# Key moments formed once and spread by a product, a later gate, another pair order and another order of loads in a gated mix of attention and gMLP

## The chip, the cores and the metric

One core of a Trainium2 chip runs the kernel. TensorE (PE) multiplies matrices into eight PSUM banks, VectorE (DVE) and ScalarE (ACT) read them, GpSimd (POOL) works on SBUF alone, and SyncE (SP) issues every transfer of this kernel in one queue. The metric is the device time of one execution in microseconds; lower is better.

## What is computed

The input x (2048 x 512) goes through two blocks, and a gate per row mixes their outputs:

```python
g = _sigmoid((x * gate_w).sum(-1, keepdims=True))
# a: attention with 32 heads of 16 for q, one shared k and v
scores = jnp.einsum('bhqd,bkd->bhqk', q, k) * Dh ** (-0.5)
o = jnp.einsum('bhqk,bkd->bhqd', _softmax(scores, axis=-1), v)
a = o.transpose(0, 2, 1, 3).reshape(B, S, H * Dh) @ wo
# b: gMLP, F = 1376, Fh = 688
z = _gelu(jnp.einsum('bsd,df->bsf', x, w_in))
z2 = _layernorm(z[..., Fh:], axis=-1)
gg = jnp.einsum('ts,bsf->btf', w_sp, z2) + b_sp[None, :, None]
b = jnp.einsum('bsf,fd->bsd', z[..., :Fh] * gg, w_out)
return g * a + (1 - g) * b
```

## The kernel before

Scores are small, so the kernel replaces exp(s) by a polynomial of third degree in s. All heads share k and v, and the sums over keys of 1, k, k k and k k k, each with and without v, are small tables, the moments. Per query only products of q with these tables are left. A guard compares the largest |q| |k| with a bound, and a general path (not run here) stands behind it.

The work is a list of tasks (`Plan.add`): engine, estimated duration, what is read and written, a priority. A planner (`Plan.run`) plays the list through with its own estimates and gives every engine a fixed order; the order of the instructions is thus set before the run, and a wait on an engine holds all that stands behind it there. `after` adds a true dependency, with its semaphore wait.

*Start.* `g_x(c)` (L551) transposes four chunks of x, 512 rows each, by TensorE into `xT`. `g_kv(c)` (L561) multiplies them with k's and v's weights and with the gate's vector as a 33rd column, and DVE forms, per key, `kx` (k), `RK` (k times v, k, v, 1) and `psi`: products of pairs of k's 16 components. There are 128 pairs (r, r+i) with i from 0 to 7, in the order r outermost (L53). POOL forms `kkE`, the pairs at distance 8, and `kkD`, a correction for the squares. `moments(c)` (L593) sums over keys: per tile of 128 keys two matmuls into bank 5 (L598, L599), and three products, each as four matmuls of 32 columns side by side with the same weights, into bank 4 (L600 to L602), so that each of four groups of 32 rows holds the same table. `moments_out` (L604) scales them into `T3`, `T3d`, `M2`, `T1b`, `T2b`, `TEb`.

*Gate.* `g_gate(c)` (L626) computes the gate once more, as rows, with weights `gwr`; `gate_out` (L631) takes the exponentials on ACT. The first gelu waits for them (`after=[ex_t[0]]`, L746), since the two functions need different tables on ACT.

*Queries.* `g_q(u)` (L640) makes q for unit u: 512 rows and 8 heads, of 16 units. q is written to DRAM (`qe`, L652; the DRAM pattern is 2 x 16 rows of 512), its first 8 rows are copied behind them (L654), and `y_load` (L659) reads it back twice for each half e of the unit: `Y` has the component r of a pair in every one of 128 partitions, `YB` the component r+i. The DRAM patterns are 16 x 8 rows of 2048.

*Units.* `unit(u)` (L671): for e in 0, 1 and j in 0 to 3, POOL multiplies Y by YB to X (L691), TensorE multiplies T3 with X (`W`, L696), DVE multiplies the result by Y to Pr (L698). M2 and T3d products of the four X, and `sel` products of the four Pr, are summed into the numerator N and the denominator D (L702 to L711). `g_den` (L717) divides and rescales for each of four row groups, `tg`.

*gMLP.* `g_z2` and `g_z1` multiply x by the two halves of w_in with gelus; layer norm on DVE, its root by a power on POOL (L752), and a normalising pass on ACT (L756). `g_sp` multiplies by the transposed w_sp, which `ld_wT` loads; `g_out` multiplies by wo and w_out and writes the rows out. z1, z2, sp and out products are the matmuls that fill TensorE while a unit waits.

Most products run as four matmuls of 32 output columns each, side by side in TensorE (`mm4`, `mmq`, L477 and L487), fewer over the whole width (`mm1`). The trace names helpers: L480, L485 and L490 are all matmuls of `mm4`, `mm1` and `mmq`.

The main list (L835 to L883): the four chunks with their moments and gates, then q for units 0 to 3, all z2, all z1, then per `tg` its four units with q four units ahead, the denominators, sp and out.

Of the kernel before, what the change touches and what calls it, by code (L numbers as in the profile page):

```python
# [17 lines left out]
D = 512  # L18
NH = 32
DH = 16  # L20
F = 1376
# [13 lines left out]
WARM = 5  # L35
# [7 lines left out]
SLACKS = {("pool", "pe"): 1200.0, ("dve", "pe"): 350.0, ("act", "pe"): 300.0}  # L43
# [3 lines left out]
DMA_ISSUE = 300.0  # L47


def constants():  # L50
# [22 lines left out]
    for e in range(2):  # L73
        for t in range(2):
            sel[p, e, t, 16 * e + 8 * t + p % 8] = 1
# [4 lines left out]
    rol = np.eye(128) + bmq * ((p[:, None] + 8) % 16 == p[None, :] % 16)  # L80
# [4 lines left out]
    small = np.concatenate([sel.reshape(128, 128), hsel.reshape(128, 128), bmq, rol], 1)  # L85
# [103 lines left out]
class Task:  # L189
    __slots__ = ("alt", "fn", "deps", "users", "left", "pri", "grp", "first", "dma", "bytes", "chan", "tag", "idx",  # L190
                 "ready", "eng", "start", "end", "op", "rate", "opens", "gates")


class Plan:
# [8 lines left out]
    def add(self, eng, cost, fn, r=(), w=(), pri=50.0, grp=None, evac=False, dma=0, size=0, chan=None, rate=DMA_RATE, tag="", after=(), opens=()):  # L203
# [5 lines left out]
        t.users, t.op, t.eng = [], None, None  # L209
        r, w = list(r), list(w)  # L210
# [16 lines left out]
        t.gates = []  # L227
        for d in t.deps:
            d.users.append(t)
        for d in t.opens:  # L230
            d.users.append(t)
        t.left = len(t.deps) + len(t.opens)
# [8 lines left out]
    def run(self, prog, allowed):  # L241
# [5 lines left out]
        pipe = [0.0]  # L247
        busy = {e: 0.0 for e in ENG}
# [9 lines left out]
        def enter(t):  # L258
            for e in t.alt:
                rt = max([0.0] + [d.end + (lat(d, e) if not (d.eng == e == "pe") else 0.0) for d in t.deps + t.opens])  # L260
                cand[e].append((rt, t))
# [29 lines left out]
        while done < len(self.tasks):  # L291
# [23 lines left out]
            for rt, t in cand[e]:  # L315
# [10 lines left out]
                k = (t.pri, t.idx)  # L326
# [4 lines left out]
            cost, fn = t.alt[e]  # L331
            t.eng = e
# [10 lines left out]
            if t.dma:  # L343
                free[e] = now + cost
                st = max(pipe[0], now + DMA_ISSUE)
                pipe[0] = st + t.bytes / t.rate
# [24 lines left out]
def build_kernel(nc, x_d, wq_d, wk_d, wv_d, wo_d, win_d, wsp_d, bsp_d, wout_d, gw_d, out_d):  # L371
    es = ExitStack()
    with es:
# [32 lines left out]
        cs = sb("cs", [128, 512], B16)  # L406
# [10 lines left out]
        T1d = sb("T1d", [128, 1], F32)  # L417
        S0 = sb("S0", [128, 1], F32)
# [45 lines left out]
        rol = cs[:, 384:512]  # L464
        x2 = x_d.rearrange("b s d -> (b s) d")
        out2 = out_d.rearrange("b s d -> (b s) d")

        def diag(t):

            a = t[:, :, :]  # L470
            return bass.AP(tensor=a.tensor, offset=a.offset, ap=[a.ap[0], [48, 2], [1, 16]])
# [4 lines left out]

        def mm4(b, n, off, lhsT, rhs, start, stop):  # L477

            def f(t):
                return [t.matmul(ps[32 * q:32 * q + 32, 512 * b() + off:512 * b() + off + n], lhsT[:, 32 * q:32 * q + 32], rhs,  # L480
                                 start=start, stop=stop, tile_position=(0, 32 * q)) for q in range(4)]
            return f

        def mm1(b, n, off, lhsT, rhs, start, stop):
            return lambda t: t.matmul(bank(b(), n, off), lhsT, rhs, start=start, stop=stop)  # L485

        def mmq(b, n, off, lhsTs, rhss, start, stop):  # L487

            def f(t):
                return [t.matmul(ps[32 * q:32 * q + 32, 512 * b() + off:512 * b() + off + n], lhsTs[q], rhss[q],  # L490
                                 start=start, stop=stop, tile_position=(0, 32 * q)) for q in range(4)]
            return f
# [8 lines left out]
        nd = [0]  # L501

        def load(eng, fn, w, r=(), size=0, n=1, pri=0.0, chan=None, rate=DMA_RATE, tag="", after=()):
# [3 lines left out]
            return add(eng, 4500.0 if rate < DMA_RATE else 540.0 * n, fn, r=r, w=w, dma=16 * n, size=size, pri=pri, chan=chan, rate=rate, tag=tag, after=after)  # L507
# [8 lines left out]
        add("dve", 350.0, lambda v: v.memset(Pr[:, 0, 0, :], 0.0), w=[("Pr", 0)], pri=-1)  # L516
        gw_ = Group("any")
# [17 lines left out]
        load("sp", lambda q: q.dma_start(win[:, :, 0:FH], win_d[:, 0:FH].rearrange("(dt p) n -> p dt n", p=128)), ["win1"], size=704512, pri=6)
        add("pool", 300.0, lambda g: g.memset(bspz[:], 0.0), w=[("bspz", 0), ("bspz", 1)], pri=0)
        add("pool", 100.0, lambda g: g.memset(nhalf[:], -0.5), w=["nhalf"], pri=0)
        add("pool", 100.0, lambda g: g.memset(RK[:, :, 304:305], 1.0), w=["rk1"], pri=0)
        add("pool", 1600.0, lambda g: g.memset(kkD, 0.0), w=[("X", c) for c in range(4)], pri=0)
# [8 lines left out]
        add("dve", 100.0, lambda v: v.tensor_copy(gwr[:], wkvg[:, :, 32:33].broadcast_to([128, 4, 32])), r=["gw"], w=["gwr"], pri=0)  # L548
# [12 lines left out]
        def g_kv(c):  # L561
            g = Group("any")
            for k in range(4):
                for dt in range(4):
                    add("pe", 26.0, mm1(lambda g=g: g.b, 33, 64 * k, xT[:, dt, 512 * c + 128 * k:512 * c + 128 * k + 128], wkvg[:, dt, 0:33], dt == 0, dt == 3),
                        r=["wk", "wv", "gw", ("x", c, dt)], grp=g, pri=0, tag="kv")
# [5 lines left out]
            add("dve", 200.0, lambda v: v.tensor_copy(RK[:, t4, 272:304].rearrange("p k (e d) -> p k e d", e=2),  # L572
                                                      src()[:, :, 16:32].unsqueeze(2).broadcast_to([128, 4, 2, 16])),
                w=[("rv", c)], grp=g, evac=True, pri=0, tag="rv")
            add("dve", 130.0, lambda v: v.tensor_scalar(RK[:, t4, 256:272], src()[:, :, 0:16], 0.25, None, ALU.mult), w=[("rk", c)], grp=g, evac=True, pri=0, tag="rk")
            add("dve", 100.0, lambda v: v.tensor_scalar(gs[:, t4].unsqueeze(2), src()[:, :, 32:33], E_MAX, None, ALU.min), w=[("gs", c)], grp=g, evac=True, pri=0, tag="gs")
            kxa = kx[:, t4, 0:16]
            kxo = bass.AP(tensor=kxa.tensor, offset=kxa.offset, ap=[kxa.ap[0], [32, 4], [1, 16], [1, 8]])
            add("dve", 620.0, lambda v: v.tensor_tensor(psi[:, t4, :].rearrange("p k (r i) -> p k r i", i=8), kxa.unsqueeze(3).broadcast_to([128, 4, 16, 8]), kxo, ALU.mult),
                r=[("kx", c)], w=[("psi", c)], pri=1, tag="psi")  # L580
            add("dve", 1150.0, lambda v: v.tensor_tensor(RK[:, t4, 0:256].rearrange("p k (c d) -> p k c d", d=16), kxa.unsqueeze(3).broadcast_to([128, 4, 16, 16]),
# [554 lines left out]
```

## Time and profile before

| | us |
|---|---|
| runs | 338.77, 335.24, 338.85 |
| median | 338.77 |
| profiled execution | 337.39 |
| its span | 335.6 |

The profile is of one execution; the span runs from the first instruction to the last. "Issue" in a chain of waits is time in which an engine waited for nothing that the profile shows. A granted clock of 1.00 is TensorE's full speed. The DMA share is the mean busy share of the core's 16 DMA engines. In a row of a group there stand the count, then busy time and mean nanoseconds of one instruction, then the engine's idle time before them and what ended it.

### The profile page before, as it was taken

To read this page: it belongs to the slowest core of one execution; us is meant where nothing else is said; L and a number is where in the kernel's file an instruction comes from. 1 tells how busy PE (TensorE), PEld (TensorE's weight loads), DVE (VectorE), ACT (ScalarE), POOL (GpSimd) and SP (SyncE) were. 2 spreads that over 40 slices of the span, in tenths; PEclk is the share of its full clock that TensorE was granted. 3 is DMA by queue.
4 is the path that set the end of the run, shared out by engine and by line. 5 is a ranking of instruction groups with operands and counts; after the bars stand their busy time and mean duration, and the time that the engine had idled before them with its cause. 6 is when DMAs were issued, how large, how long until landed. Compare 5 with 4: busy or idle time off the path is not lost.

```text
span 335.6 us, 13852 instructions
## 1 busy us (share of the span) xinstructions
PE 303.2 (90%) x6279; PEld 162.9 (49%) x6279; DVE 239.7 (71%) x335; ACT 93.8 (28%) x163; POOL 165.9 (49%) x156
## 2 busy tenths in 40 slices
PE   5976879899999997999999769988999999799993
PEld 2763345454445554564445335542565554244551
DVE  1855479998465798876949859849588977949522
ACT  2525467966655010113212002230100012000001
POOL 7421049656757284367484614376672487640000
PEclk9977899999999999999999999999999999999998
DMA  6956264999996899398999752988987579700002
GB/s 160 348 160 170 72 130 120 190 199 283 189 215 156 199 165 237 94 189 158 263 187 233 185 120 42 238 187 209 248 153 177 109 177 240 172 5 2 4 4 66
DMA packets 54472, 54.17 MB, mean 161 GB/s; under 512 B 36900, under 2 KB 45960, under 8 KB 54280
## 3 DMA queue, kind: packets, MB, share of 16 engines
q1 hardware_dynamic: 54408, 53.24, 68.6%
q8 instruction: 50, 0.82, 1.1%
q14 instruction: 14, 0.11, 0.1%
HBM read 40.65 MB, written 5.24 MB: 137 GB/s over the span
## 4 chain that ended last, share of the span: by engine, by line
PE 74%; DVE 12%; issue 6%; ACT 4%; DMA 1%; SPq 1%; DVEq 0%
PE ps L480 61%; PE ps L490 8%; DVE Pr L698 6%; PE ps L485 3%; ACT z L756 2%; PE ps L762 2%; DMA wkvg<-in_gate_w_dram 1%; ACT z L745 1%; DVE bst L747 1%; DVE z L801 1%; DVE win L735 0%; DVE nmr L753 0%; DVE Prd L713 0%; DVE Rh L728 0%; DVE outsb L828 0%
## 5 line engine op out<-in xcount | busy, mean ns | idle before, releaser
L691 POOL TENSOR_TENSOR X<-Y,YB 128x512 bf16<-128x512 bf16 x128 | 148.3, 1159 | 96.1 <-DMA Y<-qe 36.2
L698 DVE TENSOR_TENSOR Pr<-ps,Y 128x1024 bf16<-128x1024 f32 x128 | 152.3, 1215 | 32.3 <-issue 22.7
L480 PE MATMUL ps<-wT,z 128*32 128x512 bf16 x1280 | 85.0, 379 | 0.0
L480 PE MATMUL ps<-X,T 128*32 128x512 bf16 x1024 | 80.7, 380 | 4.1 <-DVE Pr L698 3.9
L480 PEld LDWEIGHTS ps<-wT,z 128*32 128x32 bf16 x1280 | 36.6, 97 | 30.0 <-issue 0.2
L480 PEld LDWEIGHTS ps<-X,T 128*32 128x32 bf16 x1024 | 26.9, 96 | 31.8 <-DVE Pr L698 12.6
L480 PE MATMUL ps<-win,xT 128*32 128x344 bf16 x512 | 25.0, 320 | 3.4 <-ACT z L745 2.9
L480 PE MATMUL ps<-wout,z 128*32 128x512 bf16 x384 | 26.2, 379 | 0.5 <-DVE z L804 0.5
L679 ACT ACTIVATE E<-ps 128x512 bf16<-128x512 f32 x16 | 9.5, 597 | 59.8 <-PE ps L480 56.1
L712 ACT ACTIVATE Ns<-ps 128x512 f32<-128x512 f32 x16 | 9.6, 599 | 58.1 <-PE ps L490 58.1
L648 ACT ACTIVATE Qt<-ps 128x512 bf16<-128x512 f32 x16 | 9.6, 597 | 47.2 <-PE ps L480 38.2
L827 ACT ACTIVATE outsb<-ps,G 128x512 bf16<-128x512 f32 x14 | 9.5, 687 | 41.5 <-PE ps L480 41.5
L480 PE MATMUL ps<-xT,win 128*32 128x512 bf16 x320 | 20.3, 380 | 0.5 <-ACT E L679 0.5
L801 DVE TENSOR_TENSOR z<-ps,z 128x512 bf16<-128x512 f32 x20 | 13.7, 683 | 9.7 <-PE ps L480 9.5
L490 PE MATMUL ps<-Pr,cs 128*32 128x512 bf16 x256 | 19.7, 379 | 0.5 <-DVE Pr L698 0.5
L735 DVE SCALAR_TENSOR_TENSOR win<-Ns,S,ps 128x512 bf16<-128x512 f32 x16 | 11.9, 745 | 10.9 <-PE ps L480 10.8
L480 PEld LDWEIGHTS ps<-win,xT 128*32 128x32 bf16 x512 | 12.6, 99 | 14.1 <-ACT z L745 7.0
L480 PE MATMUL ps<-xT,wq 128*32 128x512 bf16 x256 | 18.1, 400 | 0.6 <-ACT Q L656 0.2
L747 DVE BATCH_NORM_STATS2 bst<-z 128x6 f32<-128x344 bf16 x32 | 15.4, 505 | 4.0 <-ACT z L745 3.9
L480 PE MATMUL ps<-wo,win 128*32 128x512 bf16 x256 | 17.8, 379 | 0.0
L745 ACT ACTIVATE z<-ps 128x344 bf16<-128x344 f32 x32 | 14.0, 454 | 9.0 <-PE ps L480 7.9
L756 ACT ACTIVATE z<-z,nmr,rstd 128x688 bf16<-128x688 bf16 x16 | 15.0, 960 | 1.7 <-DVE nmr L753 1.6
(119 smaller groups left out, 314.6 us busy)
## 6 DMA issues: line engine op xcount, KB each, us to landing
Y<-qe SPq DMA_DIRECT2D x32, 512.0 KB, 5.2
YB<-qe SPq DMA_DIRECT2D x32, 512.0 KB, 6.7
wT<-in_A_x_dram SPq DMA_DIRECT2D x4, 512.0 KB, 6.1
qe<-Qt SPq DMA_DIRECT2D x64, 32.0 KB
out_dram<-outsb SPq DMA_DIRECT2D x16, 128.0 KB, 3.3
win<-in_B_w_in_dram SPq DMA_DIRECT2D x2, 688.0 KB, 8.8
qe<-qe SPq DMA_DIRECT2D x16, 64.0 KB
wout<-in_B_w_out_dram SPq DMA_DIRECT2D x1, 640.0 KB, 5.3
```

What stands on the lines that cost most here:

```text
L480: return [t.matmul(ps[32 * q:32 * q + 32, 512 * b() + off:512 * b() + off + n], lhsT[:, 32 * q:32 * q + 32], rhs, start=start, stop=stop, ...
L485: return lambda t: t.matmul(bank(b(), n, off), lhsT, rhs, start=start, stop=stop)
L490: return [t.matmul(ps[32 * q:32 * q + 32, 512 * b() + off:512 * b() + off + n], lhsTs[q], rhss[q], start=start, stop=stop, tile_position=( ...
L648: add({"act": (520.0, lambda a: a.activation(Qt[:, s, :], bank(g.b), ACT.Copy))}, 0, None, w=[("Q", s)], grp=g, evac=True, pri=1, tag="Qev")
L691: xf = lambda v, xi=xi, j=j, n=n: v.tensor_tensor(X[:, xi, :], Y[:, n % NY, j, :], YB[:, n % NYB, j, :], ALU.mult)
L698: add("dve", 1230.0, lambda v, gw=gw, pi=pi, n=n, j=j: v.tensor_tensor(Pr[:, pi, :, :], bank(gw.b, 1024).rearrange("p (t n) -> p t n", t=2 ...
L712: add({"act": (590.0, lambda a: a.activation(Ns[:, u % NNS, :], bank(gn.b), ACT.Copy))}, 0, None, w=[("Ns", u % NNS)], grp=gn, evac=True, ...
L735: add("dve", 750.0, lambda v, gr=gr, u=u, G=G: v.scalar_tensor_tensor(OT[:, tg % 2, G, :], Ns[:, u % NNS, :], S0[:, 0:1], bank(gr.b), ALU. ...
L745: add("act", 400.0, lambda a, g=g, h=h: a.activation(z2[:, FH * st + 344 * h:FH * st + 344 * h + 344], bank(g.b, 344), ACT.Gelu_apprx_tanh ...
L747: add("dve", 495.0, lambda v, h=h: v.bn_stats(bst[:, st, h, :], z2[:, FH * st + 344 * h:FH * st + 344 * h + 344]), r=[("z2", st, h)], w=[( ...
L756: add("act", 820.0, lambda a, s2=s2: a.activation(z2[:, FH * s2:FH * s2 + FH], z2[:, FH * s2:FH * s2 + FH], ACT.Identity, bias=nmr[:, s2:s ...
L801: add("dve", 690.0, lambda v: v.tensor_tensor(dst, bank(g.b), dst, ALU.mult), w=[("z1", ft, tc)], grp=g, evac=True, pri=3.5, tag="u")
```

## The change

- The moments in bank 4 are no longer formed in four copies. `RK` holds the distance-8 pairs ahead of its other columns, and a whole-width matmul takes 128 columns of it as weights: two matmuls for a key tile where three groups of four stood, and one into bank 5 where two stood. `moments_out` splits the result into two bf16 parts (`mT`) and spreads it over the partitions by six matmuls with 0/1 tables `spr`.
- The E row becomes (q_r - q_(r+8)) squared in place of the sum, `TEb` changes its sign, and the correction of the squares goes into 16 rows of M2 (`m2c`). `kkE` and `kkD` as tiles are gone; DVE or POOL may form psi and k v.
- The pairs are ordered by i first. `sel`, `psi`, T3 and both DRAM patterns of `y_load` follow: 8 x 16 rows of 2048 in place of 16 x 8.
- The gate's vector is loaded late, its column is a product of its own (`g_gs`, 64 matmuls of one column), the gate's products come after z1 in the list, the exponentials after all gelus. ACT's gelu table is asked for at the start.
- Loads: wq before x1, win1 after unit 0's loads, Q writes and Y loads with priorities of their own. `hold` only says that a task is planned after another; it replaces `after` for late loads.
- M2 and T3d products wait for the quad's last Pr. Q is computed three units ahead, two units first.
- Planner: a price for a change between four-tile and whole-width matmuls and a preference against it, a higher rate for the first loads, slack for L752 and for ACT to SP. Nine warm-up matmuls instead of five.

```diff
-    pairs = [(r, (r + i) % 16) for r in range(16) for i in range(8)]
+    pairs = [(r, (r + i) % 16) for i in range(8) for r in range(16)]
...
-                add("pe", c_mm(288), mm1(lambda: gK3.b, 288, 0, psi[:, kt, :], RK[:, kt, 0:288], st, False), r=[("psi", c), ("rkv", c), ("rk", c), ("rv", c)], grp=gK3, pri=1, tag="K3")
-                add("pe", 26.0, mm1(lambda: gK3.b, 16, 272, kkD[:, kt, :], RK[:, kt, 272:288], False, sp_), r=[("X", c), ("rv", c)], grp=gK3, pri=1, tag="K3")
-                add("pe", 30.0, mmq(lambda: gT.b, 49, 0, rep(kx[:, kt, :]), rep(RK[:, kt, 256:305]), st, False), r=[("kx", c), ("rk", c), ("rv", c), "rk1"], grp=gT, pri=1, tag="T")
-                add("pe", 26.0, mmq(lambda: gT.b, 16, 64, rep(kkE[:, kt, :]), rep(RK[:, kt, 272:288]), False, False), r=[("kkE", c), ("rv", c)], grp=gT, pri=1, tag="T")
-                add("pe", 26.0, mmq(lambda: gT.b, 1, 96, rep(RK[:, kt, 272:304]), rep(RK[:, kt, 304:305]), False, sp_), r=[("rv", c), "rk1"], grp=gT, pri=1, tag="T")
+                add("pe", c_mm(288), mm1(lambda: gK3.b, 288, 0, psi[:, kt, :], RK[:, kt, 16:304], st, sp_), r=[("psi", c), ("rkv", c), ("rk", c), ("rv", c)], grp=gK3, pri=1, tag="K3")
+
+                add("pe", 30.0, mm1(lambda: gT.b, 49, 0, RK[:, kt, 193:321], RK[:, kt, 272:321], st, False), r=[("rkv", c), ("rk", c), ("rv", c), "rk1"], grp=gT, pri=1, tag="T")
+                add("pe", 26.0, mm1(lambda: gT.b, 16, 49, RK[:, kt, 0:128], RK[:, kt, 288:304], False, sp_), r=[("kkE", c), ("rkv", c), ("rv", c)], grp=gT, pri=1, tag="T")
...
+            for i, (off, lo, n) in enumerate(((0, 0, 49), (64, 49, 16), (96, 48, 1))):
+                for z in range(2):
+                    add("pe", 30.0, lambda t, i=i, off=off, lo=lo, n=n, z=z: t.matmul(bank(gT2.b, n, off), spr[:, i, :], mT[:, z, lo:lo + n], start=i == 0 and z == 0, stop=i == 2 and z == 1),
+                        r=["cs", "mTh", "mTl"], grp=gT2, pri=1, tag="T2")
...
+        def g_gs(st):
+            for dt in range(4):
+                add("pe", 26.0, mm1(lambda: gS.b, 1, st, xT[:, dt, 128 * st:128 * st + 128], wkvg[:, dt, 32:33], dt == 0, dt == 3), r=["gw", ("x", st // 4, dt)], grp=gS, pri=22, tag="gate")
...
-            load("sp", lambda q: q.dma_start(Y[:, n % NY, :, :].rearrange("p j n -> p (j n)"), dap(qe, o0, [[QP, 16], [0, 8], [1, 2048]])), [("Y", n % NY)], r=[("qe", u)],
-                 size=524288, pri=10 + u + 0.1 * e, chan="y%d" % (n % NY), tag="Y")
-            yld[0] = load("sp", lambda q: q.dma_start(YB[:, n % NYB, :, :].rearrange("p j n -> p (j n)"), dap(qe, o0, [[QP, 16], [QP, 8], [1, 2048]])), [("YB", n % NYB)], r=[("qe", u), ("qx", u)],
-                 size=524288, pri=10 + u + 0.2 * e, chan="yb%d" % (n % NYB), tag="YB")
+            load("sp", lambda q: q.dma_start(Y[:, n % NY, :, :].rearrange("p j n -> p (j n)"), dap(qe, o0, [[0, 8], [QP, 16], [1, 2048]])), [("Y", n % NY)], r=[("qe", u)],
+                 size=524288, pri=YPRI + u + 0.1 + 0.4 * e, chan="y%d" % (n % NY), tag="Y")
+            yld[0] = load("sp", lambda q: q.dma_start(YB[:, n % NYB, :, :].rearrange("p j n -> p (j n)"), dap(qe, o0, [[QP, 8], [QP, 16], [1, 2048]])), [("YB", n % NYB)], r=[("qe", u), ("qx", u)],
+                 size=524288, pri=YPRI + u + 0.2 + 0.4 * e, chan="yb%d" % (n % NYB), tag="YB")
...
-                add("pe", c_mm(512), mmq(lambda: gn.b, 512, 0, [M2[:, e, :]] * 4, [X[:, i, :] for i in xs], False, False), r=["M2"] + xr, grp=gn, pri=pr_, tag="N")
+                add("pe", c_mm(512), mmq(lambda: gn.b, 512, 0, [M2[:, e, :]] * 4, [X[:, i, :] for i in xs], False, False), r=["M2"] + xr, grp=gn, pri=pr_, tag="N", after=tp[3:])
```

More of the change, by code (lines that the diff above doesn't have):

```diff
@@ L34 @@
 SLACK = 1.016
-WARM = 5
+WARM = 9
 QP = 4096 + 256
@@ L190 @@
     __slots__ = ("alt", "fn", "deps", "users", "left", "pri", "grp", "first", "dma", "bytes", "chan", "tag", "idx",
-                 "ready", "eng", "start", "end", "op", "rate", "opens", "gates")
+                 "ready", "eng", "start", "end", "op", "rate", "opens", "gates", "tiles", "slack")
 class Plan:
@@ L226, in add @@
         t.opens = [self.lastw[k] for k in opens]
-        t.gates = []
+        t.gates = list(hold)
+        t.slack = slack
         for d in t.deps:
             d.users.append(t)
-        for d in t.opens:
+        for d in t.opens + t.gates:
             d.users.append(t)
-        t.left = len(t.deps) + len(t.opens)
+        t.left = len(t.deps) + len(t.opens) + len(t.gates)
         for k in r:
@@ L247, in run @@
         pipe = [0.0]
+        tiles = 1
         busy = {e: 0.0 for e in ENG}
@@ L325, in run @@
                     continue
-                k = (t.pri, t.idx)
+                k = (t.pri + (SWITCH_PRI if e == "pe" and t.tiles != tiles else 0.0), t.idx)
                 if best is None or k < best[0]:
@@ L331, in run @@
             cost, fn = t.alt[e]
+            if e == "pe":
+                if t.tiles != tiles:
+                    cost += SWITCH
+                tiles = t.tiles
             t.eng = e
@@ L345, in run @@
                 st = max(pipe[0], now + DMA_ISSUE)
-                pipe[0] = st + t.bytes / t.rate
+                pipe[0] = st + t.bytes / (DMA_FIRST if st < 16000.0 and t.rate == DMA_RATE else t.rate)
                 t.end = pipe[0] + DMA_LAT
@@ L475, in build_kernel, with mm1 @@
         add = pl.add
+        def mm1(b, n, off, lhsT, rhs, start, stop):
+            return lambda t: t.matmul(bank(b(), n, off), lhsT, rhs, start=start, stop=stop)
         def mm4(b, n, off, lhsT, rhs, start, stop):
@@ L481, in f @@
                                  start=start, stop=stop, tile_position=(0, 32 * q)) for q in range(4)]
+            f.tiles = 4
             return f
-        def mm1(b, n, off, lhsT, rhs, start, stop):
-            return lambda t: t.matmul(bank(b(), n, off), lhsT, rhs, start=start, stop=stop)
         def mmq(b, n, off, lhsTs, rhss, start, stop):
@@ L501, in build_kernel, with load @@
         nd = [0]
-        def load(eng, fn, w, r=(), size=0, n=1, pri=0.0, chan=None, rate=DMA_RATE, tag="", after=()):
+        yld = [None]
+        def load(eng, fn, w, r=(), size=0, n=1, pri=0.0, chan=None, rate=DMA_RATE, tag="", after=(), hold=()):
             if chan is None:
@@ L516, in build_kernel @@
         add("dve", 350.0, lambda v: v.memset(Pr[:, 0, 0, :], 0.0), w=[("Pr", 0)], pri=-1)
+        add("act", 1300.0, lambda a: a.activation(nmr[:, 0:1], ones[:, 0:1], ACT.Gelu_apprx_tanh), r=["ones"], w=["junk2"], pri=-2, tag="table")
         gw_ = Group("any")
@@ L863, in build_kernel @@
             g_z2(st)
-        for ft in range(6):
-            for tc in range(4):
-                g_z1(ft, tc)
         for tg in range(4):
@@ L870, in build_kernel @@
                 unit(u)
-                if u < 2:
-                    ld_wT(u)
+                if u == 0:
+                    ld_win1()
+                    for ft in range(6):
+                        for tc in range(4):
+                            g_z1(ft, tc)
+                    load("sp", nonc(lambda q: q.dma_start(wkvg[:, :, 32:33], gw_d.rearrange("(dt p one) -> p dt one", p=128, one=1))), ["gw"], size=16384, pri=20, hold=[yld[0]])
+                    add("dve", 100.0, lambda v: v.tensor_copy(gwr[:], wkvg[:, :, 32:33].broadcast_to([128, 4, 32])), r=["gw"], w=["gwr"], pri=20, tag="gate")
+                    for c in range(4):
+                        g_gate(c)
+                    for st in range(NST):
+                        g_gs(st)
+                    gate_out()
+                    q_and_guard(2)
+                if u in (1, 3):
+                    ld_wT(u // 2)
                 if u == 2:
                     ld_late()
-                if u + 4 < 16:
-                    q_and_guard(u + 4)
+                if u + 3 < 16:
+                    q_and_guard(u + 3)
             g_den(tg)
```

160 lines of the change are left out of this document (85 added, 75 removed).

## The prediction

> **What bounds the kernel now.** I read the page first: the shares, the slices, the queues, the chain.
>
> ```profile
> span 335.6 us, 13852 instructions
> PE 303.2 (90%) x6279; PEld 162.9 (49%) x6279; DVE 239.7 (71%) x335; ACT 93.8 (28%) x163; POOL 165.9 (49%) x156
> ...
> PEclk9977899999999999999999999999999999999998
> ...
> q1 hardware_dynamic: 54408, 53.24, 68.6%
> q8 instruction: 50, 0.82, 1.1%
> ...
> PE 74%; DVE 12%; issue 6%; ACT 4%; DMA 1%; SPq 1%; DVEq 0%
> ```
>
> TensorE is busy for 90% and carries 74% of the chain: the kernel is bound by matmuls, and a gain must come from time in which TensorE works badly or not at all. The profiled run took 337.39 us, of which the span is 335.6; the median of the three runs is 338.77, 1.4 above it. My sum is made against 337.4.
>
> Then the table by stretches tells where TensorE loses time.
>
> ```profile
> core 0: us, PE busy (x) PEld busy (x) DVE busy (x) ACT busy (x) POOL busy (x), PEclk, DMA share, GB/s
> 10.00:20.00 10.00, 8.17 (x207) 6.24 (x206) 7.75 (x17) 4.87 (x10) 3.63 (x4) 0.96 0.77 256
> 20.00:30.00 10.00, 7.57 (x240) 5.68 (x237) 5.99 (x14) 3.96 (x7) 3.19 (x4) 0.84 0.67 185
> 30.00:40.00 10.00, 8.38 (x128) 4.01 (x132) 5.21 (x23) 4.76 (x10) 0.00 (x0) 0.68 0.46 121
> 40.00:50.00 10.00, 7.66 (x184) 3.75 (x172) 6.37 (x17) 6.04 (x13) 3.38 (x4) 1.00 0.51 110
> 41.00:42.00 1.00, 0.84 (x20) 0.45 (x24) 0.10 (x1) 0.86 (x3) 0.00 (x0) 1.00 0.13 46
> 119.00:121.00 2.00, 2.00 (x56) 1.20 (x52) 1.96 (x3) 0.53 (x2) 1.65 (x2) 1.00 0.93 272
> 50.00:295.00 245.00, 230.74 (x4718) 121.00 (x4722) 192.42 (x234) 69.15 (x120) 146.22 (x127) 1.00 0.82 183
> ```
>
> From 50 to 295 us TensorE idles for 14.3 of 245 us. From 10 to 50 it idles for 8.2 of 40, and where it is busy the granted clock was 0.84 in one stretch and 0.68 in the next. So the time to be won lies in the first 50 us. The chain of waits and the timeline say what stands there.
>
> ```profile
> 2.79 4.65 DMA wkvg<-in_gate_w_dram
> ...
> 16.76 1.83 issue
> ...
> 27.57 3.13 issue
> ```
>
> ```profile
> 7.46 0.45 DVE L548 COPY gwr<-wkvg 128x128 bf16<-128x128 bf16 x1 [3.78 <-DMA wkvg<-in_gate_w_dram]
> ...
> 10.71 0.68 PE L485 MATMUL ps<-wkvg,xT 128*128 128x33 bf16 x13
> ...
> 13.71 0.64 PE L490 MATMUL ps<-wT 128*32 128x16 bf16 x48
> ...
> 24.96 0.49 PE L480 MATMUL ps<-win,xT 128*32 128x344 bf16 x8
> ...
> 27.05 1.28 ACT L745 ACT_TABLE_LOAD   x1
> ...
> 29.63 1.20 SPq L664 DMA_DIRECT2D YB<-qe  x2
> ...
> 46.23 1.04 POOL L752 TENSOR_TENSOR rstd<-ve,nhalf 128x4 f32<-128x4 f32 x1 [19.51 <-DVE ve L751]
> ...
> 47.50 4.85 POOL L691 TENSOR_TENSOR X<-Y,YB 128x512 bf16<-128x512 bf16 x4 [0.23 <-POOL rstd L752]
> ```
>
> The two "issue" gaps are waits of TensorE for nothing that the profile shows, both inside the run of small moment matmuls. My reading, not shown by these rows: its instructions had not arrived (the q8 row is their fetch, 0.82 MB in 50 packets). The first z2 matmuls stand at 24.96, since their gelu may run only after the gate's exponentials. GpSimd stood for 19.5 us behind an early L752, so the first X came at 47.50.
>
> **The change, part by part.**
>
> *Moments.* Per key tile there were 1 + 1 + 4 + 4 + 4 = 14 matmuls (L598 to L602), now 3, for 16 tiles: 176 fewer, each with its weight load.
>
> ```profile
> L485 PE MATMUL ps<-wT,X 128*128 128x16 bf16 x16 | 2.8, 187 | 0.0
> ...
> L490 PE MATMUL ps<-wT 128*32 128x49 bf16 x64 | 2.6, 186 | 0.0
> ...
> L490 PE MATMUL ps<-wT 128*32 128x1 bf16 x64 | 2.4, 166 | 1.8 <-issue 1.8
> ...
> L490 PE MATMUL ps<-wT 128*32 128x16 bf16 x64 | 2.2, 174 | 3.1 <-issue 3.1
> ...
> L618 DVE SCALAR_TENSOR_TENSOR T2b<-ps,cs 128x128 bf16<-128x128 f32 x1 | 0.3, 292 | 3.1 <-PE ps L490 3.1
> ```
>
> A run of 48 small ones took 0.64 us, 53 ns for each four. Three fours per tile go (159 ns) and two single ones come, at 34 to 52 ns by the 0.68 us for 13 L485 matmuls: about 65 ns saved, and some 30 ns for the 16-column product; 16 x 95 = -1.5 us. With the run three times shorter I let both gaps go: -5.0. (If they come back elsewhere: 0.) The low clock follows them: 10 x 0.16 + 10 x 0.32 = 4.8 us of clock are lost in the two stretches; I take all of it back as part of the same step, -4.8, lower end 0, since work then also finds fewer free slots. [...]
>
> *The spread.* Six matmuls over `mT` with two DVE steps before them lengthen the way from moments to T1b, T2b, TEb. By a small DVE step of this kernel (L618 below) that is two times 0.3 us and the matmuls, about 1 us; z2 matmuls hide it. Without that cover +1.
>
> *Gate late.* The scalar load of 512 single elements held DVE until 7.46 us, and its copy took 0.45; the xT copies behind it (from 7.60) stood ready for about as long: -0.7, lower end 0, upper -1.2. The gate's 64 four-tile matmuls only move. The one column that rode along in the key/value product becomes 64 matmuls of its own: 64 x 34 to 52 ns = 2.2 to 3.3; +2.5. They stand in the full stretch, so nothing hides them. The exponentials and their 1.28 us table load move to ACT behind the last gelu; ACT is busy for 69 of 245 us there, and the first reader is far behind: 0. Its cover gone, +2.
>
> *Longer warm-up.* Four more matmuls while TensorE waits for x: 0.
>
> *Order of loads, POOL.* wq before x1 delays x1 by one 512 KB load, but the gate's load is gone and win1 is moved away; L752 is no longer ahead of X.
>
> ```profile
> SPq L165 <- DVE Pr L698: 58.5, 17, 9.5
> ...
> SPq L652 <- ACT Q L656: 34.6, 10, 13.3
> ```
>
> The first YB was issued at 29.63, behind a write of Qt that itself waited; the queue lost 34.6 us in such waits. Now the loads of units 0 and 1 come ahead of the later Q writes, and wq arrives earlier: I put the first YB at about 19 us, a head start of 11 us for the loads, and the first X some 15 to 20 us earlier. A wait of SP for a Q that is late now delays Y and YB behind it, as before. Its worth is only that TensorE has more to choose from; 0, lower end -4.
>
> *N and D of a quad in one run.* M2 and T3d products now wait for the fourth Pr (1215 ns, L698 below). z1, sp and out work is queued to fill in; X buffers come free later, while GpSimd idles for 96 us before L691 (its row below). 0; without cover a quarter of a Pr for each of 32 quads, +10; in the best case -2.
>
> *Staying in one tiling.* I see no idle time at changes of tiling in the rows above; 0 to -2, taken as 0.
>
> *Y and YB by another order.* This is the part that can cost.
>
> ```profile
> L691 POOL TENSOR_TENSOR X<-Y,YB 128x512 bf16<-128x512 bf16 x128 | 148.3, 1159 | 96.1 <-DMA Y<-qe 36.2 <-PE ps L490 27.2 <-PE ps L480 24.8
> L698 DVE TENSOR_TENSOR Pr<-ps,Y 128x1024 bf16<-128x1024 f32 x128 | 152.3, 1215 | 32.3 <-issue 22.7 <-PE ps L480 8.6 <-PE ps L490 0.4
> ...
> Y<-qe SPq DMA_DIRECT2D x32, 512.0 KB, 5.2
> YB<-qe SPq DMA_DIRECT2D x32, 512.0 KB, 6.7
> ...
> qe<-Qt SPq DMA_DIRECT2D x64, 32.0 KB
> ```
>
> The bytes stay, but the DRAM side goes from 16 rows of 8 to 8 of 16. In 41 to 42 us only the writes of Qt (L652) are in flight; their DRAM pattern begins with a dimension of 2, and the share is 0.13, that is 2 of 16 engines, at 46 GB/s, 23 each. In 119 to 121 Y loads run, whose pattern begins with 16: share 0.93, 272 GB/s, 18.3 per engine. So a pattern that begins with 8 should use 8 engines. From 50 to 295 us 183 x 245 = 44.8 MB are moved, of which 58 Y and YB loads are 30.4 MB. The eight engines would carry 30.4/8 + 14.4/16 = 4.70 MB each, and the two that also write Qt (2.1 MB) 5.62. They have 245 + 11 = 256 us. At 23 GB/s the two need 244 us, at 18.3 they need 307: 0 to +51. Below nothing I see no reason. I take 23, since eight engines ask for less in all (184 GB/s) than the 272 that pass now; but at 95% use some waits for Y must come: +2.
>
> [...]
>
> Sum: 337.4 - 1.5 - 5.0 - 4.8 - 0.7 + 2.5 + 2 = 329.9; I say 330.
>
> **The rivals.**
>
> *A. The loads become the bound (slower).* Place: POOL X L691 waiting for Y and YB, already 36.2 us now. It begins where an engine under load moves less than 5.62 MB / 256 us = 22.0 GB/s, and eats the gain of 9.5 us at 5.62/265.5 = 21.2. Between that and today's 18.3 (middle 19.7: 285 us, +29) the time is 337.4 - 9.5 + 29 = 357; at 18.3 it is 379. For: 16 engines do only 18.3 now, and the matmul order is fixed, so a late Y stalls TensorE. Against: half as many engines compete.
>
> *B. The loads cost nothing* (16 engines after all, or hidden), and the earlier X saves its 4 us as well: 337.4 - 9.5 - 4 = 324.
>
> *C. The start does not shorten:* ACT, with 16 normalising passes and 32 gelus early, ends the waits at 40 to 70 us whatever comes before. Then -1.5 - 0.7 + 2.5 + 2: 339.7, no change.
>
> **How the numbers follow.** The likeliest, 330, has 0.45, with its own range 324 to 338. A has 0.32, B 0.17, C 0.06. About 1% (335.4 to 342.2 around 338.8) is what a measurement of this kernel tells from no change. Faster: 0.33 of the likeliest's 0.45, all of B: 0.50. Same: 0.10 of the likeliest and 0.04 of C: 0.14. Slower: A, and 0.04 of the rest: 0.36. The range of 8 in 10 runs from 316 (B with the gaps of 50 to 295 us shortened as well) to 370; what is left out is the upper part of A, 0.13, and little below.
>
> **What would show it.** Right: no "issue" gap among the moment matmuls, clock near 1.00 from 20 to 40 us, z2 before 20 us, X before 35 us, DMA share near 0.5 while Y alone is moving, at 180 GB/s or more. Wrong: Y's and YB's median time to landing far above 5.2 and 6.7 us with GpSimd's waits for them far above 36 us (A); a share of 0.9 in Y loads (B); TensorE still idling some 8 us between 10 and 50 (C).

## The result and the profile after

| | us, median | runs |
|---|---|---|
| before | 337.0 | 334.8 to 338.85, 4 runs |
| after | 404.07 | 400.1 to 407.04, 4 runs |

The ratio is 1.189, with a 95% interval of 1.173 to 1.206: the change makes the kernel 67 us slower, and the forecast of 330 and its range of 316 to 370 both miss it. (A fifth execution of the changed kernel on record took 411.94.) The profiled execution took 406.93 us, of which the span is 405.1. Here and below a ratio leaves disturbed runs out and a median doesn't, so the two can differ by a per cent.

The page of the changed kernel; its parts come in the same order as those shown of before.

```profile
span 405.1 us, 13651 instructions
PE 328.0 (81%) x6177; PEld 176.5 (44%) x6177; DVE 237.7 (59%) x333; ACT 94.3 (23%) x164; POOL 165.6 (41%) x155
...
PEclk9996998999999988898979999899899877979998
...
q1 hardware_dynamic: 53896, 53.34, 70.7%
q8 instruction: 49, 0.80, 0.9%
...
PE 37%; SPq 23%; DMA 20%; issue 7%; POOL 6%; DVE 3%; ACT 2%; DVEq 0%; POOLq 0%
...
L717 POOL TENSOR_TENSOR X<-Y,YB 128x512 bf16<-128x512 bf16 x128 | 148.0, 1156 | 192.6 <-DMA Y<-qe 89.9
L724 DVE TENSOR_TENSOR Pr<-ps,Y 128x1024 bf16<-128x1024 f32 x128 | 152.9, 1219 | 91.4 <-PE ps L498 74.1
```

TensorE's share of the chain that ended last fell from 74% to 37%; transfers and SP's queue have 43% of it, where they had 2%. As many bytes are moved as before (53.34 MB in q1 against 53.24). The clock strip falls below 9 in slices all over the span, not at its start alone. The span is 69.5 us longer: TensorE idles for 44.7 us more (77.1 against 32.4) and is busy for 24.8 us more (328.0 against 303.2), with 102 matmuls fewer, at a granted clock of 0.92 on the mean against 0.98.

The waits (who waits for what: us in total, times, longest) say who pays:

```profile
POOL X L717 <- DMA Y<-qe: 89.9, 16, 8.7
...
PEld ps L498 <- issue: 53.4, 93, 4.5
...
PE ps L498 <- POOL X L717: 31.8, 15, 7.5
...
PE ps L498 <- issue: 18.0, 12, 4.3
...
POOL X L717 <- DMA YB<-qe: 12.9, 1, 12.9
```

GpSimd waited 36.2 us for Y before, and none for YB; now it waits 102.8 us for both. From issue to the last landing a load of Y or YB took 6.1 us at the median before and 10.8 now, by its semaphore's updates. Before, no idle stretch of TensorE of more than 0.25 us ended with an X; now those ahead of the W products sum to 31.8 us. The "issue" waits of TensorE have grown as well, from 9.1 to 27.4 us in stretches of more than 0.25 us: they are a second cost, and the last section reads them.

The table by stretches, with the columns as before (the last three: granted clock, DMA share, GB/s):

```profile
10.00:20.00 10.00, 9.42 (x177) 6.23 (x175) 9.85 (x18) 6.56 (x13) 6.11 (x7) 1.00 0.53 172
20.00:30.00 10.00, 7.93 (x149) 3.91 (x147) 7.13 (x28) 5.50 (x11) 1.77 (x2) 1.00 0.71 154
30.00:40.00 10.00, 4.01 (x56) 1.98 (x60) 2.20 (x4) 0.46 (x1) 4.81 (x5) 0.66 0.57 137
...
50.00:350.00 300.00, 244.29 (x4598) 131.77 (x4594) 181.41 (x226) 68.49 (x115) 134.25 (x117) 0.93 0.83 145
...
339.00:341.00 2.00, 2.00 (x34) 1.56 (x28) 1.18 (x2) 0.00 (x0) 0.00 (x0) 0.75 0.50 123
```

The last row is the one to keep: from 339 to 341 us only rows of Y and YB are moving (every packet in it has 4096 bytes), two loads at a time. The share is 0.50, that is 8 of 16 engines, and they move 123 GB/s, 15.4 each. (The share adds up the times of packets, and those of one engine can overlap, since it passes 1 in a row of e1 below; so it counts engines only where one kind of packet is moving.) The packets say the same: whenever any of 4096 bytes are under way, 16 at a time was the commonest number before, and 8 is now. The early part did as forecast: no "issue" gap of more than 0.45 us stands among the moment matmuls, the first row's clock is 1.00, and the first z2 matmul stands at 16.11 us. Then the first X waits for its load:

```profile
34.79 4.85 POOL L717 TENSOR_TENSOR X<-Y,YB 128x512 bf16<-128x512 bf16 x4 [12.94 <-DMA YB<-qe]
```

### The profile page after: what moved, and what is told of

It reads as the page before. It is cut to its first block, busy times and chain, and to the rows that moved or that the text cites. A ratio compares the mean times of both kernels' runs of the same rounds, so it can differ in the third digit from the quotient of the medians.

```text
span 405.1 us, 13651 instructions
## 1 busy us (share of the span) xinstructions
PE 328.0 (81%) x6177; PEld 176.5 (44%) x6177; DVE 237.7 (59%) x333; ACT 94.3 (23%) x164; POOL 165.6 (41%) x155
## 3 DMA queue, kind: packets, MB, share of 16 engines
q1 hardware_dynamic: 53896, 53.34, 70.7%
## 4 chain that ended last, share of the span: by engine, by line
PE 37%; SPq 23%; DMA 20%; issue 7%; POOL 6%; DVE 3%; ACT 2%; DVEq 0%; POOLq 0%
PE ps L498 32%; DMA Y<-qe 14%; SPq L808 12%; POOL X L717 6%; SPq L678 6%; PE ps L506 4%; DMA YB<-qe 3%; DVE Pr L724 2%; DMA wq<-in_A_wq_dram 1%; PE ps L789 1%; SPq L688 1%; DMA qe<-Qt 1%; SPq L690 1%; SPq L680 1%; DVE win L762 1%
## 5 line engine op out<-in xcount | busy, mean ns | idle before, releaser
L498 PE MATMUL ps<-X,T 128*32 128x512 bf16 x1024 | 89.8, 408 | 45.0 <-POOL X L717 31.8
L498 PE MATMUL ps<-wT,z 128*32 128x512 bf16 x1280 | 89.6, 396 | 2.9 <-issue 2.9
L498 PEld LDWEIGHTS ps<-X,T 128*32 128x32 bf16 x1024 | 29.5, 101 | 73.5 <-POOL X L717 26.9
L498 PEld LDWEIGHTS ps<-wT,z 128*32 128x32 bf16 x1280 | 37.9, 101 | 36.7 <-issue 9.7
L498 PE MATMUL ps<-win,xT 128*32 128x344 bf16 x512 | 25.6, 337 | 5.5 <-issue 4.9
L498 PE MATMUL ps<-wout,z 128*32 128x512 bf16 x384 | 29.4, 401 | 0.5 <-DVE z L831 0.5
L498 PE MATMUL ps<-xT,win 128*32 128x512 bf16 x320 | 21.8, 380 | 2.4 <-issue 2.2
L498 PE MATMUL ps<-wo,win 128*32 128x512 bf16 x256 | 21.8, 410 | 0.1
L506 PE MATMUL ps<-Pr,cs 128*32 128x512 bf16 x256 | 21.7, 396 | 0.0
L498 PEld LDWEIGHTS ps<-win,xT 128*32 128x32 bf16 x512 | 14.1, 105 | 16.5 <-issue 5.4
L774 DVE BATCH_NORM_STATS2 bst<-z 128x6 f32<-128x344 bf16 x32 | 15.8, 505 | 8.4 <-ACT z L772 8.4
L498 PE MATMUL ps<-xT,wq 128*32 128x512 bf16 x256 | 19.5, 401 | 1.0 <-DMA wq<-in_A_wq_dram 0.8
L740 DVE SCALAR_TENSOR_TENSOR Prd<-ps,T1d,Qt 128x512 bf16<-128x512 f32 x16 | 12.0, 747 | 13.2 <-PE ps L506 13.1
L789 PE MATMUL ps<-wT,z 128*32 128x256 bf16 x256 | 10.5, 287 | 9.5 <-issue 9.5
L498 PEld LDWEIGHTS ps<-wout,z 128*32 128x32 bf16 x384 | 14.1, 103 | 9.1 <-issue 2.1
```

Source lines behind the costliest of these rows:

```text
L740: add("dve", 750.0, lambda v: v.scalar_tensor_tensor(Prd[:, u % NPD, :], bank(gd.b), T1d[:, 0:1], Qt[:, s, :], ALU.add, ALU.mult), r=["T1d ...
L774: add("dve", 495.0, lambda v, h=h: v.bn_stats(bst[:, st, h, :], z2[:, FH * st + 344 * h:FH * st + 344 * h + 344]), r=[("z2", st, h)], w=[( ...
```

## The experiments

**Is it the engines of the loads? (e1, e2, e3)** Each kernel gets the other's DRAM patterns, and nothing else. In e1 the changed kernel reads by 16 rows of 8 again (in the diffs of this section long lines are shortened to the part that changes):

```diff
-dap(qe, o0, [[0, 8], [QP, 16], [1, 2048]])     # Y
+dap(qe, o0, [[QP, 16], [0, 8], [1, 2048]])
-dap(qe, o0, [[QP, 8], [QP, 16], [1, 2048]])    # YB
+dap(qe, o0, [[QP, 16], [QP, 8], [1, 2048]])
```

> The changed kernel with one edit: the DRAM patterns of the Y and YB loads begin with 16 again, as before. Y then holds another component of q than its pairs ask for, so the attention part of the output is another function; the number, size and order of all instructions are those of the changed kernel. Theory E (the loads run on 8 of 16 DMA engines, and all else of the change is a small gain): 325 us, 318 to 335; DMA share of lone Y loads near 0.9, Y lands in about 5 us, GpSimd's wait for Y falls from 89.9 us to under 45. Rival O (the new order of matmuls and loads, with N and D held back to the quad's end, made the loss): 380 us or more. Rival half: each has a part, 345 to 375.

Measured 332.31 us (10 runs, 330.13 to 340.1), ratio to before 1.0005, 0.993 to 1.008. The whole loss is gone, and a gain is not shown either. GpSimd's waits for the loads, and TensorE's for issue, in e1:

```profile
POOL X L717 <- DMA Y<-qe: 8.8, 2, 6.0
...
POOL X L717 <- DMA YB<-qe: 6.8, 1, 6.8
PE ps L498 <- issue: 5.3, 4, 2.1
```

e2 is the reverse edit of the kernel before (8 rows of 16).

> The kernel before with one edit: the DRAM patterns of Y and YB begin with 8, as in the changed kernel (8 x 16 rows of 2048). Y holds other components than its pairs ask for, so the attention part of the output is another function; the order of all instructions is that of before. Theory E: the edit alone makes the loss, 400 us, 380 to 425, with Y alone in flight at a DMA share near 0.5. Rival O: 335 to 350, since the old order hides the loads.

394.48 us (386.77 to 400.27) against 335.99: 58 us of loss from these two lines alone, with nothing else of the change. The waits are those of the changed kernel, 109.2 us of GpSimd for Y where there were 36.2:

```profile
POOL X L691 <- DMA Y<-qe: 109.2, 22, 12.1
...
PE ps L480 <- POOL X L691: 15.5, 13, 3.4
```

e3 gave the kernel before a pattern of 8 x 2 x 8 rows (`[[2 * QP, 8], [QP, 2], [0, 8], [1, 2048]]`).

> The kernel before with the same rows in the same places, but the DRAM patterns written as 8 x 2 x 8 rows, so that they begin with 8 while each engine reads other rows than its neighbours; the output is unchanged. Theory E (the number of engines alone): within 3% of the run with 8 x 16 rows. Rival S (in the changed kernel all engines read the same row of Y at the same time, and that row's DRAM is the limit): 340 to 365, at least 8% below the run with 8 x 16 rows, though 8 engines are used.

336.02 us, ratio 0.996 (0.981 to 1.010). This run told nothing of its question: the first two dimensions are one dimension of 16 in steps of QP, and each load gave 16 updates of its semaphore, as before; in the changed kernel, at the share of 0.50, each gives 9. Its rival S, that engines which read the same row at once are slow, can be judged by the packets of the other runs: one of 4096 bytes took 261 ns on the mean in the kernel before, where by its pattern an engine repeats one row of its own in Y's loads, and 241 in the changed kernel and 227 in e2, where all eight go through the same rows. So shared rows were not slower, and nothing here speaks for S.

**Can the rest of the change be kept? (e4)** The changed kernel with the old order of pairs and 16-engine loads; the correction of the squares, which the new order put into 16 partitions, is spread to every eighth by a fourth 0/1 table:

```diff
-    pairs = [(r, (r + i) % 16) for i in range(8) for r in range(16)]
+    pairs = [(r, (r + i) % 16) for r in range(16) for i in range(8)]
...
-            sel[p, e, t, 16 * e + 8 * t + p // 16] = 1
+            sel[p, e, t, 16 * e + 8 * t + p % 8] = 1
...
+    spr[np.arange(16), 3, 8 * np.arange(16)] = 1
...
-            for i, (off, lo, n) in enumerate(((0, 0, 49), (64, 49, 16), (96, 48, 1))):
+            for i, (off, lo, n) in enumerate(((0, 0, 49), (64, 49, 16), (96, 48, 1), (112, 49, 16))):
```

> The changed kernel with the pair order of before (component outermost), so that both loads begin with 16, and the correction of the squares spread to every eighth partition by two more small matmuls; all else of the change is kept and all of the computation is done. Theory E: within 1.5% of the first run of this list, about 325 us, faster than before by 2 to 5%. Rival O: 380 us or more.

334.79 us, ratio 0.996 (0.988 to 1.004): the loss is gone here too, but the 2 to 5% of gain that was expected did not come.

**How do eight engines cost 60 to 70 us? (e5, e6)** e5 puts only Y's loads of the changed kernel back on 16 engines (the first pair of lines of e1's diff). e6 leaves the loads and spreads the writes of q:

```diff
-return [q.dma_start(dap(qe, o0 + 512 * j, [[2048, 2], [QP, 16], [1, 512]]), Qt[32 * j:32 * j + 32, s, :]) for j in range(4)]
+return [q.dma_start(dap(qe, o0 + 512 * j + 2048 * a, [[QP, 16], [1, 512]]), Qt[32 * j + 16 * a:32 * j + 16 * a + 16, s, :]) for j in range(4) for a in range(2)]
```

> The changed kernel with Y's rows in the order of before (all 16 engines) and YB's left on eight; the cross-products pair other rows, so the attention output is another function, with the same instructions on every engine. Theory E, a ceiling (a busy engine carries a 4-KB row in about 257 ns, and nothing is lost until the two busiest engines are full): they would carry 32 loads of 8 rows and 32 of 16, 32 x 2.1 + 32 x 4.1 = 198 us, and some 92 us of writes of Q and the rest as before, 290 us in all, less than TensorE's work: 328 to 345 us. Rival L, each load on eight engines costs its own share of the loss, since it lands late whatever the total: half of the loss of 70 us stays, 360 to 378 us.

> The changed kernel with each write of Q in eight transfers of 16 partitions in place of four of 32 that begin with a dimension of 2, so that 16 engines share it and not two; all else, the order of every engine too, is the same, and the full computation stands. Theory E2, that the two engines which also carry Q are the ones that bound: their 47 us of Q writes become 6, and the time falls by 30 to 45 us, to 358 to 375 us. Rival M, all eight engines of the loads bound (or the queue of SP, which now has 128 more issues at about 0.6 us each): within 8 us of the changed kernel, 396 to 412 us.

e5 took 364.09 us (354.23 to 369.63; ratio 1.088, 1.077 to 1.099), the number of L and not of E (for E's 257 ns a row the means are 261 before and 241 in the changed kernel). e6 took 387.86 (381.93 to 389.53), 16 us below the changed kernel: between both expectations (it gives SP 64 more issues, not the 128 that rival M names). The waits explain why neither is a plain hit. Those of e5, of TensorE for issue and of GpSimd for the loads:

```profile
PE ps L498 <- issue: 17.5, 10, 3.1
...
POOL X L717 <- DMA Y<-qe: 22.7, 5, 7.6
...
POOL X L717 <- DMA YB<-qe: 9.5, 1, 9.5
```

The same of e6:

```profile
POOL X L717 <- DMA Y<-qe: 80.7, 15, 10.3
...
PE ps L498 <- issue: 38.6, 14, 9.0
```

In e5 the loads are in time again, nearly as E said, but TensorE's waits for issue stay as long as in the changed kernel. In e6 the loads of Y are late about as often as in the changed kernel, though X holds TensorE less, and the waits for issue in the row of L498 have doubled (18.0 to 38.6 us). I summed from the traces every idle stretch of TensorE over 0.25 us by what ended it:

| | ended by X | by issue | granted clock | median us |
|---|---|---|---|---|
| before | 0 | 9.1 | 0.98 | 337.0 |
| after | 31.6 | 27.4 | 0.92 | 404.1 |
| e1 | 1.4 | 5.3 | 0.98 | 332.3 |
| e2 | 15.8 | 22.2 | 0.94 | 394.5 |
| e5 | 4.1 | 23.3 | 0.97 | 364.1 |
| e6 | 6.3 | 41.8 | 0.94 | 387.9 |
| e13 | 42.1 | 9.3 | 0.94 | 388.0 |
| e15 | 15.7 | 7.9 | 0.97 | 355.9 |

So the two lines of the loads cost TensorE twice: in e2 the idle time that an X ended grew from 0 to 15.8 us, and the issue waits from 9.1 to 22.2 (the last section). The granted clock falls at such gaps: of the 13 stretches at a clock of 0.50 in the changed kernel, of 3.4 to 10.2 us, 12 begin in or just behind a gap of 2.1 to 9.5 us, and 11 of these gaps ended with an X or with issue. All but the medians come from one profiled execution each; that of e5 was its shortest run, 354.23 us, and that of e13 its longest, 395.97.

**Full engines, or a blocked queue? (e13, e14, e15)** In the changed kernel SP's own rows show another suspect:

```profile
298.01 14.92 SPq L808 DMA_TRANSPOSE wT<-in_B_w_sp_dram  x1
...
316.41 15.71 SPq L808 DMA_TRANSPOSE wT<-in_B_w_sp_dram  x1
332.21 0.59 SPq L688 DMA_DIRECT2D Y<-qe  x1
332.91 0.57 SPq L690 DMA_DIRECT2D YB<-qe  x1
```

SP stands 15.7 us in issuing one transposing load, and Y and YB go out only then. Over all 16 transposes these holds sum to 166 us, against 67 before. e13 makes them plain loads of the same bytes, which leaves w_sp untransposed (another function at the same sizes), e14 does so in the kernel before, e15 is e13 with e6's writes of q.

```diff
-q.dma_start_transpose(wT[:, tc % 2, :, 128 * k:128 * k + 128], wsp_d[r0:r0 + 128, :])
+q.dma_start(wT[:, tc % 2, :, 128 * k:128 * k + 128], wsp_d[r0:r0 + 128, :].rearrange("p (k n) -> p k n", n=128))
```

> The changed kernel with the 16 transposing loads of the spatial weights (512 KB each) made plain loads of the same bytes in packets of 256 bytes, so the spatial product is computed with untransposed weights; the order of every engine and queue is the same. In the changed kernel SP stood 166 us in issuing the 16 transposes (67 us before), with loads of Y and YB queued behind. Theory T, that the transposes' hold of the queue makes the loads late: 340 to 365 us, SP free within 1 us of each issue. Rival E, that the eight engines are full whatever SP does: 385 to 405 us, the waits of POOL for Y and YB stay above 80 us.

> The kernel before with the same replacement (untransposed spatial weights), the control for e13. Both theories: SP's 67 us of holds were hidden there, 328 to 338 us; anything the plain loads take off here is to be taken off e13 as well.

> e13 with the writes of Q on 16 engines as in e6 (untransposed spatial weights). Theory T: hardly below e13, 338 to 362 us. Rival E: the two engines that carry Q are relieved, so 15 to 35 us below e13, 355 to 385 us.

e13 took 387.95 us (ratio 1.160, 1.127 to 1.193), e14 336.66 (1.013, 0.998 to 1.028), e15 355.88 (352.24 to 364.65). Rival E's times are met in e13 and e15, and e14, the control, shows no gain of the edit by itself. The holds of the transposes fell from 166 to 29.5 us, and the waits of GpSimd in e13 show Y later than ever:

```profile
POOL X L717 <- DMA Y<-qe: 131.7, 22, 10.4
```

So the holds were not the main cause of the late loads; why an issue stands for 15.7 us is not shown. The 16 us that e13 did win did not come from the loads: TensorE's idle time that X ended grew from 31.6 to 42.1 us, while its issue waits fell from 27.4 to 9.3. Relieving the two engines that also carry q (the share of 0.13 in the row of 41 to 42 us before) gave 32 us there, inside the 15 to 35 that E asked for.

**Where did the gain go? (e7 to e12)** e7 and e8 start from e4. e7 drops the bind of N and D behind the quad's four products; e8 instead sets the planner's price on a change of tiling to 0. e9 drops the bind from e1. From e7, e10 spreads the writes of q as e6 does, e11 drops the price too, and e12 issues each YB load only when its Y has landed (`after=[yt]`).

```diff
-[X[:, i, :] for i in xs], False, False), r=["M2"] + xr, grp=gn, pri=pr_, tag="N", after=tp[3:])
+[X[:, i, :] for i in xs], False, False), r=["M2"] + xr, grp=gn, pri=pr_, tag="N")
...
-SWITCH = 100.0
-SWITCH_PRI = 2.0
+SWITCH = 0.0
+SWITCH_PRI = 0.0
```

> The kernel of e4 (old order of pairs, loads on 16 engines, correction of the squares spread by two more matmuls) without the bind that puts N and D of a quad behind the quad's four products in one run. Full computation. Theory G, that the bind gives back the 10 us that the start saves, because N and D wait for the fourth product while work behind them in TensorE's queue stands: 324 to 330 us, and the lost time of TensorE behind 50 us falls by 4 us or more. Rival H, that what is given back lies in instruction fetch and in the half clock behind its gaps, wherever these fall: within 1% of e4, 331 to 338 us.

> The kernel of e4 without the planner's price on TensorE's change from one shape of matmul to another (SWITCH and SWITCH_PRI at 0), so that the runs of W products are shorter and N and D mix in again. Full computation. If the switch price is what gives the start's gain back: 324 to 330 us; if the price is worth something by itself: 337 to 345 us; rival H, as in the run before: within 1% of e4, 331 to 338 us.

> The kernel of e1 (the changed kernel with Y's and YB's rows on 16 engines, so the attention output is another function) without the bind of N and D behind the quad's four products. The same question as e7, on the other order of pairs. Theory G, that the bind costs some 5 us by itself: 325 to 330 us against e1's 332.3, ratio to the kernel before 0.975 to 0.99. Rival H, that the difference of e7 to e4 came of fewer late instruction fetches in those runs and has nothing to do with the bind: 330 to 336 us, ratio 0.99 to 1.01.

> The kernel of e7 with the writes of Q on 16 engines (eight transfers of 16 partitions each, as in e6). Full computation. If the two engines that carry Q also delay loads or instruction fetches where the loads run on 16: 1 to 4 us below e7, 325 to 328 us. If not, or if 64 more issues on SP cost as much as they save: 328 to 334 us.

> The kernel of e7 with the planner's price on a change of matmul shape at 0, so that N, D and the W products mix as in the kernel before. Full computation. If the longer runs of one shape are worth something: 331 to 336 us. If not: within 1% of e7, 326 to 332 us.

> The kernel of e7 with each YB load issued only when the Y load of its pair has landed, so that fewer loads are under way at a time (e7 had 1.1 on the mean between 40 and 290 us, the kernel before 1.45, the changed kernel 2.1). Full computation. Theory F, that TensorE's instruction fetches are late because they wait for the transfers under way: the waits of TensorE put down to issue fall from 4.5 to below 3 us, and the time stays at 326 to 331 us unless X waits take their place. Rival X, the loads come too late: waits of POOL for YB above 40 us in all and 333 us or more. If issue waits do not fall with fewer loads under way, F falls.

| | us, median | ratio to before | bind |
|---|---|---|---|
| e1 | 332.31 | 1.0005 (0.993 to 1.008) | yes |
| e4 | 334.79 | 0.996 (0.988 to 1.004) | yes |
| e8 | 333.06 | 0.997 (0.993 to 1.002) | yes |
| e7 | 329.14 | 0.981 (0.974 to 0.988) | no |
| e9 | 331.16 | 0.989 (0.984 to 0.994) | no |
| e10 | 329.01 | 0.982 (0.976 to 0.988) | no |
| e11 | 328.44 | 0.984 (0.978 to 0.989) | no |
| e12 | 341.61 | 1.022 (1.017 to 1.027) | no |

Apart from e12, which costs by itself, the interval of every kernel without the bind lies below 1, and that of none with it does. Three pairs differ in the bind alone (e7 and e4, e9 and e1, e11 and e8): dropping it is worth 1.2 to 1.5% in each by the ratios, 4 to 5 us, about half of what the start saves; by the medians it is 5.7, 1.2 and 4.6 us. The planner makes a new order for each of them, so this is the price of the bind together with the order that it brings. e9 is the least clear: its time fell where H wanted it and its ratio where G did. Why the bind costs is not shown. TensorE's idle time behind 50 us falls in all three pairs, from 22.2 to 17.3, from 19.3 to 12.6 and from 21.8 to 18.0 us, as G has it; but most of the fall is issue waits, as H has it (8.6 to 4.5, 5.3 to 0.5, 5.2 to 2.4), and these scatter as much between single profiled runs (5.9 in e10, without the bind). The price on tiling is worth nothing that these runs can tell, and where the loads use 16 engines the writes of q cost nothing either. e7, e10 and e11 beat both kernels, by 1.6 to 2% on the kernel before, and cannot be told from each other.

In e12 theory F falls as it was put. The loads under way went down to 1.09 on the mean from e7's 1.33 (the 1.1 that was put down for e7 leaves out the loads of one semaphore, of whose 176 updates 9 are missing from the trace), and the issue waits were 5.3 us against 4.5, by one profiled execution of each. Rival X holds: the loads come too late, by the waits of GpSimd in e12:

```profile
POOL X L716 <- DMA YB<-qe: 77.1, 11, 14.4
```

## Why the prediction was wrong

**The step that failed** is in *Y and YB by another order*: "I take 23, since eight engines ask for less in all (184 GB/s) than the 272 that pass now". That the loads would use 8 engines was right (share 0.50, 9 updates for a load). But the rate did not follow the total: with half as many engines asking, each moved 15.4 GB/s in the row of 339 to 341 us, and not more than the 18.3 it moved beside fifteen others. Over all packets of 4096 bytes (8320 in either kernel) the means of 261 ns before and 241 now are 15.7 and 17.0 GB/s: hardly faster for half the engines. Why such a row takes that long is not shown. The 23 came from the writes of q, another kind of transfer: packets of 1024 bytes from SBUF to DRAM, where the loads read rows of 4096 bytes from DRAM. The row of 119 to 121 us was the nearest in kind, and it was there. The 3.8 MB of Y and YB rows that fall on each engine (30.4 MB over eight) take 247 of the 256 us by themselves at 15.4, and 224 at 17.0, before the writes of q and the rest. With 17.0 in place of 23 the prediction's own working gives 5.62 MB in 331 us, 75 more than there are, and 337.4 - 9.5 + 75 = 403 us. That this comes so near to 404 is partly luck, since the issue waits, 27.4 us, are not in it; but it shows the size of the term: +2 stood where e2 measured 58.

**Rival A was the right mechanism**, at the place it named: GpSimd's X waits for Y and YB, and 15.4 to 17.0 lie below the 21 to 22 GB/s under which its loss was to begin. Its price was too low: 357, or 379 at 18.3. Two parts of it were in no term: a rate below 18.3, and TensorE's issue waits, which the prediction priced only in the first 50 us.

**The start** was sized well. In e1, where the loads don't disturb, TensorE idles for 2.7 us from 10 to 50 us where it idled for 8.2, at a clock of 0.89 in the first stretch and 1.00 behind it, by its table by stretches:

```profile
10.00:20.00 10.00, 10.00 (x175) 7.04 (x176) 9.43 (x20) 7.21 (x14) 5.38 (x5) 0.89 0.50 160
20.00:30.00 10.00, 9.06 (x166) 4.39 (x163) 7.70 (x26) 5.04 (x10) 3.35 (x4) 1.00 0.99 250
30.00:40.00 10.00, 8.64 (x212) 5.09 (x204) 8.87 (x19) 4.43 (x10) 8.95 (x8) 1.00 0.55 150
40.00:50.00 10.00, 9.56 (x228) 5.12 (x224) 9.49 (x23) 8.60 (x17) 5.97 (x7) 1.00 1.11 208
```

5.5 us of idling and some 4.1 of clock came back (5.2 lost in these four rows before, 1.1 now), 9.6 together, against -5.0, -4.8 and -0.7 forecast. But "both gaps go" was true of their place alone: e1 waits 5.3 us for issue elsewhere, so "if they come back elsewhere: 0" was the better half of that term.

**N and D of a quad in one run** was put at 0, with +10 if uncovered; the runs make it 4 to 5 us (e7, e9 and e11 against e4, e1 and e8). The cover named for it was work on TensorE; what uncovers it stays open. Staying in one tiling was put at 0, and e8 and e11 agree. Moments (-1.5), the gate's column (+2.5) and the spread were not run by themselves; the column's 64 matmuls are busy for 2.1 us in the changed kernel.

**C fell** by the rows above. **B fell** by the 0.50.

## What to carry to other kernels

Before a pattern of a transfer is turned round, read from a row in which such a transfer moves alone how many engines it uses (here 16 x 8 rows ran at a share of 0.93, 8 x 16 rows at 0.50, writes that begin with 2 at 0.13), and price them with a rate per engine from a row of the same kind of transfer, not from the total. When a queue's issue stands for many microseconds, free it in a run before it is taken for the cause: here its holds fell from 166 to 29.5 us, and that won 16 of 67 us (e13). And part a bundled change: one of its seven parts cost some 60 us and another 4 to 5, and without both the rest is worth 2%.

## What was not expected of the hardware

TensorE's "issue" gaps keep to places in its stream. Of 96 such gaps of more than 0.45 us in all 17 kernels, 92 stand 192 to 194 above a multiple of 256 in TensorE's stream of matmuls and weight loads (indices 449, 962, 4801 and 7361 in the kernel before); the other four are one and the same place in e1, e5, e6 and e15. And 83 end 1.2 to 1.7 us after a packet of 16 KB on queue q8, which the page calls "instruction", has landed, all 14 of the kernel before and the changed one among them; for the two gaps that the prediction names it is 1.46 and 1.34 us. From these two counts I estimate that the gaps are late instructions; no trace shows an instruction's arrival. The longest stands in the changed kernel, here in its timeline (start and us, engine, line, and in brackets the idle time before):

```profile
332.21 0.59 SPq L688 DMA_DIRECT2D Y<-qe  x1
332.81 4.84 POOL L717 TENSOR_TENSOR X<-Y,YB 128x512 bf16<-128x512 bf16 x4 [8.18 <-DMA Y<-qe]
332.91 0.57 SPq L690 DMA_DIRECT2D YB<-qe  x1
336.05 1.47 PE L789 MATMUL ps<-wT,z 128*32 128x256 bf16 x22 [9.46 <-issue]
```

The packet ahead of it ran from 333.86 to 334.79 us, and TensorE went on at 336.05. Take a block to be 256 instructions from one such index to the next. In order of time each packet stands ahead of one block, which begins at least 1.2 us after the landing. Counted from TensorE's entry into the block two ahead of it, the packet landed after 9.5 us at the median in the kernel before and 11.9 in the changed one, one in ten after more than 12.1 and 17.4 us; two blocks last 13 and 16 us on the mean. With nothing but the two lines of the loads changed, TensorE's issue waits grew from 9.1 to 22.2 us (e2). By the same estimate, then, loads on 8 engines delayed instructions as well as X. Whether the packet waits, and behind what, is not shown: with plain loads in place of the transposes the issue waits fell from 27.4 to 9.3 us where the loads use 8 engines (e13), and hardly where they use 16 (8.8 in e14, 9.1 before).
